# Moving parts of an on-chip float64 conversion from GpSimd to VectorE in a planned attention-and-MLP kernel

## The chip, the cores and the metric

The kernel runs on one core of a Trainium2 chip. The metric is device time in microseconds (us); three runs of the kernel before gave a median of 1079.98 us (1079.9 to 1080.02). The profile shows five engines of the core: TensorE (PE, with its weight loads as PEld), VectorE (DVE), ScalarE (ACT), GpSimd (POOL) and SyncE (SP), which here only issues transfers.

## The reference

A linear attention in the manner of Performer, followed by a two-layer MLP with an ELU between the layers. The attention's inputs are float32. The two weight matrices of the MLP come as float64.

```python
batch, n_heads, seq, head_dim = 8, 8, 576, 64      # 4608 tokens, 128 features
def phi(x):                                        # x is q or k, scaled
    h = einsum('bhsd,md->bhsm', x, omega) - sum(x * x, -1, keepdims=True) / 2
    return exp(h - max(h, -1, keepdims=True)) / sqrt(m)
kv  = einsum('bhsm,bhsd->bhmd', k_p, v)            # k_p = phi(k), q_p = phi(q)
z   = sum(k_p, axis=2)
x   = einsum('bhsm,bhmd->bhsd', q_p, kv) / (einsum('bhsm,bhm->bhs', q_p, z)[..., None] + 1e-06)
# x becomes 4608 x 512, heads side by side
h   = x @ w_in                                     # 512 x 2048
g   = where(h > 0, h, exp(min(h, 0)) - 1)
out = g @ w_out                                    # 2048 x 512
```

## The kernel before

**Attention** is done by pairs of heads, 32 pairs (`i` from 0), four to a batch entry. A pair's k is projected into `ppk` (the transposes and products on PE; minimum, exponent and so on elsewhere), its features are `hk`; `kv` multiplies them with v into `pkv` and sums them into `z`; q is projected into `ppq`, its features are `hq`. `finish` spreads z over the partitions (`pz`), forms the denominators on VectorE (L652 and the reciprocal at L661, tile `den`), divides `hq` by them ("norm", a tensor_tensor at L350), transposes it on PE (`pt`, L673), copies it to `qh`, multiplies with kv into `pn` (L700), and splits the result into a high part `xh` (ScalarE) and a low part `xl` (VectorE, L713). The first pairs project plain float32 x in four-pass matmuls (L457); from pair 7 of k and pair 8 of q on, x is split first into two parts (`tk`, `tq`; a tensor_tensor at L350) and projected by L507.

**MLP.** The tokens are worked in 12 blocks of 384; d_ff is worked in 16 steps of 128. A step F of layer 1 takes 12 matmuls (L830 to L832: high times high, high times low, low times high, for four chunks of 128 of the model's width) into `ph`, ScalarE and VectorE make the ELU `e` (L839, L840, L843), and `e` is split into `g`, high (a copy at L345 or L347) and low (a tensor_tensor at L350). Layer 2 multiplies g with w2 into three accumulators, nine matmuls for a step (L864 to L866). Blocks 0 to 2 are done in two halves of d_ff each, the rest whole. Block 0 needs the pairs 0 to 3; block 1 needs the pairs 4 to 7 as well, the chunk c of its steps the pair 4 + c.

**Conversion.** The weights are 32 tiles of 128x512 float64 words (16 of w1, 16 of w2). `from_f64` loads a tile into `raw` (L752, 512 KB), ScalarE scales its upper word into `u` (L755) and its lower one in place (L759), then come a clamp (L763, a tensor_scalar on VectorE or GpSimd), a shift (L770) and a sign (L775) on VectorE, an integer add on GpSimd (L778), the high part (a copy by ScalarE or VectorE, L345 or L347, into `w1c` or `w2h`) and the low part, the tail (`w1c` or `w2l`, a tensor_tensor at L350). w1's two parts are also written to DRAM (`w1s`, L802) for the later blocks, which load them from there (L805). Step f of block 0 needs w1's tile f, and its layer 2 w2's tile f.

**Order.** Nothing is ordered by hand. Every operation is recorded with an engine, a duration by a formula, a due time and its dependencies (`op`), and `Plan.order` deals them out: each engine, when free, starts the earliest due operation that is ready. Some operations carry alternatives (`alt`); `ALT` says how many us later (or earlier, if negative) the other engine is taken to be. `mine` decides whether the engine that asks should have the operation. The planner also holds VectorE and GpSimd apart for operations marked `port` (`held`). Each tag of `Buf` has a number of buffers, and a tile waits for one of them to come free. The kernel then runs each engine's list in that order, each instruction waiting on semaphores for its inputs.

Of the kernel before, what the change touches and what calls it, by code (L numbers as in the profile page):

```python
# [98 lines left out]
class Plan:  # L99
# [167 lines left out]
ALT = dict(kv=1, out=2, conv_clamp=-1, conv_hi=-1, conv_sub=2, g_hi=0, g_lo=1, y_hi=None, y_lo=-1, norm=2, turn=2, x_hi=2, sq=0)  # L267
# [24 lines left out]
def performer_elu_kernel(  # L292
# [102 lines left out]
    def load_pair(i, due):  # L395
# [7 lines left out]
        for nm, nat, mixed in (("k", k, kx), ("q", q, qx)):  # L403
            if native(i, nm):
                t = s["x" + nm] = Buf(sb, [P, 2, S], F32, "ld" if nm == "k" else "t", f"x{nm}_{i}", 2)
# [174 lines left out]
    def kv_sums(i, due, p, parts):  # L580
# [25 lines left out]
        def add(n, d, dst, x, y, reads):  # L606
            op("POOL", pool(n), d, lambda: nc.gpsimd.tensor_tensor(dst(), x(), y(), ALU.add), reads, (z,))

        add(4 * M, due + 0.1, lambda: z(), lambda: h()[:, 0:4], lambda: h()[:, 4:8], parts)
        add(2 * M, due + 0.2, lambda: z()[:, 0:2], lambda: z()[:, 0:2], lambda: z()[:, 2:4], (z,))  # L610
        for a in range(2):
# [3 lines left out]
                lambda r=r: h()[r, 8], [*parts, z],  # L615
            )

    def finish(i, due):
# [110 lines left out]
    def from_f64(src, hi, lo, nm, due, key):  # L729
# [19 lines left out]
        def ui():  # L749
# [13 lines left out]
            lambda e: (nc.vector if e == "DVE" else nc.gpsimd).tensor_scalar(  # L763
                u(), u(), -F64_MAX, F64_MAX, ALU.max, ALU.min
            ),
# [250 lines left out]
```

## Time and profile before

| | |
|---|---|
| median of three runs | 1079.98 us |
| the profiled execution | 1078.17 us, of which a span of 1076.3 us between first and last instruction |
| PE, ACT, DVE, POOL busy | 1050.0, 731.6, 601.5, 474.4 us |
| mean granted clock of TensorE | 0.99 |

The profile's groups name a line, an engine, an operation and its tiles (output first), then the count, the busy time, the mean duration of one in ns and the idle time of the engine before it with what ended it. Where a line is that of a helper (L345 and L347 for copies, L350 for every tensor_tensor by `tt`), the tile names tell the operations apart. Two records stand in the trace for one float32 matmul of the projections and of the products with kv.

### The profile page before, as it was taken

The numbers are of one execution on the slowest core, as the hardware profiler recorded it, in microseconds if no ns is written. First come the engines' busy times: TensorE is split into PE (matmuls) and PEld (weight loads), VectorE is DVE, ScalarE is ACT, GpSimd is POOL, SyncE is SP. The second block draws the span as 40 slices with busy tenths as digits, with TensorE's granted clock in tenths as the row PEclk, the third lists the DMA queues.
The fourth block names the chain that finished last, engine by engine and source line by source line (L and its number), as shares of the span: only waits on it lengthen the run. The fifth ranks groups of instructions, "written<-read, shape, count | busy, mean of one in ns | idle before, by whom it ended". The sixth has DMA issues, their size and how long they took to land.

```text
span 1076.3 us, 19179 instructions
## 1 busy us (share of the span) xinstructions
PE 1050.0 (98%) x6043; PEld 916.2 (85%) x6043; DVE 601.5 (56%) x2343; ACT 731.6 (68%) x1949; POOL 474.4 (44%) x466
## 2 busy tenths in 40 slices
PE   7999699999999999999999999999999999999998
PEld 7777589898888888998888888898888888898987
DVE  5788889755776754235666665224566665322221
ACT  6987775547977985347889998427899988432222
POOL 4677666753443554223454345223344554322221
PEclk8999899999999999999999999999999999999999
DMA  6555477657553553435455545444545542253431
GB/s 196 155 178 191 166 255 258 227 211 234 187 194 128 185 170 128 166 118 168 170 169 156 170 150 177 149 135 134 180 138 177 167 153 98 98 167 131 153 125 62
DMA packets 53237, 176.92 MB, mean 164 GB/s; under 512 B 6032, under 2 KB 6224, under 8 KB 53136
## 3 DMA queue, kind: packets, MB, share of 16 engines
q1 hardware_dynamic: 53136, 175.69, 49.3%
q8 instruction: 49, 0.80, 0.3%
q14 instruction: 52, 0.43, 0.1%
HBM read 155.48 MB, written 20.19 MB: 163 GB/s over the span
## 4 chain that ended last, share of the span: by engine, by line
PE 83%; ACT 5%; DVE 5%; DMA 3%; POOL 2%; issue 2%; SPq 0%; POOLq 0%; DVEq 0%; ACTq 0%
PE acc L864 12%; PE ph L830 11%; PE acc L866 11%; PE acc L865 11%; PE ph L832 11%; PE ph L831 11%; PE ppq L507 2%; PE pt L673 2%; PE pkv L591 2%; PE pn L700 2%; PE ppk L507 2%; DMA xk<-in_kx_dram 1%; PE ppq L457 1%; ACT hk L427 1%; ACT hq L427 1%
## 5 line engine op out<-in xcount | busy, mean ns | idle before, releaser
L350 POOL TENSOR_TENSOR g<-e,g 128x384 fp32r<-128x384 f32 x176 | 186.4, 1059 | 450.5 <-DVE g L347 333.3
L830 PE MATMUL ph<-xh,w1c 128*128 128x384 f32 x768 | 266.6, 347 | 0.8 <-DVE e L843 0.8
L832 PE MATMUL ph<-xh,w1c 128*128 128x384 f32 x768 | 258.3, 336 | 0.0
L831 PE MATMUL ph<-xl,w1c 128*128 128x384 f32 x768 | 258.0, 336 | 0.0
L843 DVE SCALAR_TENSOR_TENSOR e<-e,ph 128x384 f32<-128x384 f32 x192 | 106.2, 553 | 247.5 <-ACT e L840 244.0
L839 ACT ACTIVATE e<-ph 128x384 f32<-128x384 f32 x192 | 94.7, 493 | 216.1 <-PE ph L832 209.7
L864 PE MATMUL acc<-w2h,g 128*128 128x512 f32 x576 | 235.1, 408 | 0.7 <-ACT o L345 0.7
L865 PE MATMUL acc<-w2l,g 128*128 128x512 f32 x576 | 228.3, 396 | 0.0
L866 PE MATMUL acc<-w2h,g 128*128 128x512 f32 x576 | 228.2, 396 | 0.0
L830 PEld LDWEIGHTS ph<-xh,w1c 128*128 128x128 f32 x768 | 144.5, 188 | 15.6 <-issue 5.1
L831 PEld LDWEIGHTS ph<-xl,w1c 128*128 128x128 f32 x768 | 144.6, 188 | 8.0
L832 PEld LDWEIGHTS ph<-xh,w1c 128*128 128x128 f32 x768 | 144.0, 188 | 0.0
L866 PEld LDWEIGHTS acc<-w2h,g 128*128 128x128 f32 x576 | 108.6, 189 | 25.7
L864 PEld LDWEIGHTS acc<-w2h,g 128*128 128x128 f32 x576 | 108.6, 189 | 17.6 <-issue 4.1
L865 PEld LDWEIGHTS acc<-w2l,g 128*128 128x128 f32 x576 | 108.9, 189 | 11.7
L840 ACT ACTIVATE e<-e 128x384 f32<-128x384 f32 x192 | 101.6, 529 | 3.4
L525 DVE CUSTOM_DVE_ANT_0 hq<-ppq,p2q 128x128 f32<-128x128 f32 x216 | 54.1, 288 | 63.4 <-ACT p2q L516 62.4
L350 POOL TENSOR_TENSOR hq<-hq,den 128x512 f32<-128x512 f32 (+1 forms) x93 | 81.0, 884 | 10.2 <-DVE den L661 8.5
L525 DVE CUSTOM_DVE_ANT_0 hk<-ppk,p2k 128x128 f32<-128x128 f32 x225 | 56.3, 287 | 45.6 <-ACT p2k L516 41.1
L652 DVE CUSTOM_DVE_ANT_0 junk<-hq,pz 128x128 f32<-128x128 f32 (+1 forms) x320 | 73.5, 280 | 10.6 <-PE pz L633 8.2
L516 ACT ACTIVATE p2q<-ppq,sqq 128x128 f32<-128x128 f32 x216 | 67.5, 369 | 14.0 <-PE ppq L507 13.3
L516 ACT ACTIVATE p2k<-ppk,sqk 128x128 f32<-128x128 f32 x225 | 67.4, 365 | 7.1 <-PE ppk L507 6.9
(94 smaller groups left out, 1619.5 us busy)
## 6 DMA issues: line engine op xcount, KB each, us to landing
w1c<-w1s SPq DMA_DIRECT2D x176, 512.0 KB, 3.3
raw_w<-in_w_dram SPq DMA_DIRECT2D x32, 512.0 KB, 4.2
xk<-in_kx_dram SPq DMA_DIRECT2D x25, 576.0 KB, 4.2
xq<-in_qx_dram SPq DMA_DIRECT2D x24, 576.0 KB, 4.6
v<-in_v_dram SPq DMA_DIRECT2D x32, 325.0 KB, 3.6
out_dram<-o SPq DMA_DIRECT2D x36, 256.0 KB, 2.6
w1s<-w1c SPq DMA_DIRECT2D x16, 512.0 KB, 3.3
xq<-in_q_dram SPq DMA_DIRECT2D x8, 288.0 KB, 3.9
```

The lines of the kernel that those rows point to most:

```text
L350: (nc.vector if e == "DVE" else nc.gpsimd).tensor_tensor(*args)
L516: nc.scalar.activation(p2()[:, a], view()[:, a, M:], AF.Identity, bias=sq()[:, j:j + 1], scale=1.0)
L525: nc.vector.tensor_tensor_reduce(out=h()[:, j, :], in0=view()[:, a, 0:M], in1=p2()[:, a, :], scale=1.0, scalar=HIGHEST, op0=ALU.add, op1=A ...
L830: nc.tensor.matmul(ph(), wh, xh[:, c, o:o + TB], start=(c == 0), stop=False)
L831: nc.tensor.matmul(ph(), wh, xl[:, c, o:o + TB], start=False, stop=False)
L832: nc.tensor.matmul(ph(), wl, xh[:, c, o:o + TB], start=False, stop=(c == NC - 1))
L839: op("ACT", act(TB, True), due, lambda: nc.scalar.activation(e(), ph(), AF.Relu, scale=-1.0), (p,), (e,))
L840: op("ACT", act(TB), due + 0.2, lambda: nc.scalar.activation(e(), e(), AF.Exp, scale=-1.0), (e,), (e,))
L843: lambda: nc.vector.scalar_tensor_tensor(e(), e(), -1.0, ph(), ALU.add, ALU.max), (p, e), (e,),
L864: nc.tensor.matmul(a(), g()[:, 0, ts], w2h[:, f], start=(f == f0), stop=False)
L865: nc.tensor.matmul(a(), g()[:, 0, ts], w2l[:, f], start=False, stop=False)
L866: nc.tensor.matmul(a(), g()[:, 1, ts], w2h[:, f], start=False, stop=(f == f1 - 1))
```

## The change

Seven edits in one:

- The clamp of the conversion is VectorE's alone; before, GpSimd could take it.
- The conversion's tail goes to VectorE first; GpSimd takes it only if that ends 1 us sooner by the planner's reckoning. Before, it was GpSimd's, with VectorE 2 us behind.
- The low part of `g` in block 0's steps goes to VectorE first; in the other blocks it stays GpSimd's first.
- `mine` now counts the time for which the other of VectorE and GpSimd holds the two apart.
- `raw` has four buffers, not three. The z sums of the pairs from 8 on, and the kv that is transposed there, which had two buffers of their own each, now lie in buffers of `raw`.
- The x of k (and the x of q that is split) has three buffers, not two.
- `qh`, the turned q, has one buffer, not two.

Line numbers of the changed kernel are some 5 to 14 higher: L457 is L462 there, L507 L512, L673 L686, L700 L713, L713 L726, L763 to L778 are L776 to L788, L830 to L832 are L840 to L842, L843 is L853, L864 to L866 are L878 to L880, and the helpers L345, L347 and L350 are L350, L352 and L355.

```diff
 # Plan.order, mine(n, eng): when would the other engine e end this operation?
-                t = max(free[e], now, ready[n][e]) + ns + late * 1e3
+                t = max(free[e], now, ready[n][e])
+                if e == "POOL":
+                    t = max(t, held["DVE"])
+                elif e == "DVE" and tasks[n][6]:
+                    t = max(t, held["POOL"])
+                t += ns + late * 1e3
...
-ALT = dict(kv=1, out=2, conv_clamp=-1, conv_hi=-1, conv_sub=2, g_hi=0, g_lo=1, y_hi=None, y_lo=-1, norm=2, turn=2, x_hi=2, sq=0)
+ALT = dict(kv=1, out=2, conv_hi=-1, conv_sub=1, g_hi=0, g_lo=1, g_lo0=1, y_hi=None, y_lo=-1, norm=2, turn=2, x_hi=2, sq=0)
...
 # load_pair: x of k, x of q
-                t = s["x" + nm] = Buf(sb, [P, 2, S], F32, "ld", f"x{nm}_{i}", 2)
+                t = s["x" + nm] = Buf(sb, [P, 2, S], F32, "ld", f"x{nm}_{i}", 3)
...
 # kv_sums: z and the kv to be transposed
-        z = s["z"] = Buf(sb, [P, 4, M], F32, "zs", f"zs_{i}", 2)
-        kvt = Buf(sb, [P, M], F32, "kvt", f"kvt_{i}", 2)
+        zt = s["z"] = Buf(sb, [P, 2 * 512], I32, "raw", f"zs_{i}", 4)
+        ktk = (zt, "kvt")
...
 # finish
-        qh = Buf(sb, [P, 2, S], F32, "qh", f"qh_{i}", 2)
+        qh = Buf(sb, [P, 2, S], F32, "qh", f"qh_{i}", 1)
...
 # from_f64
-        raw = Buf(sb, [P, 2 * 512], I32, "raw", f"raw_{nm}", 3)
+        raw = Buf(sb, [P, 2 * 512], I32, "raw", f"raw_{nm}", 4)
...
             "DVE", dve(512, True), due - 6,
-            lambda e: (nc.vector if e == "DVE" else nc.gpsimd).tensor_scalar(
-                u(), u(), -F64_MAX, F64_MAX, ALU.max, ALU.min
-            ),
-            (u,), (u,), alt=other("conv_clamp", "POOL", 1885), port=True,
+            lambda: nc.vector.tensor_scalar(u(), u(), -F64_MAX, F64_MAX, ALU.max, ALU.min), (u,), (u,), port=True,
...
-            "POOL", pool(512), due - 3,
+            "DVE", dve(512), due - 3,
             lambda e: tt(e, lo(), u(), hi().bitcast(F32), ALU.subtract), (u, key + ("h",)), (key + ("l",),),
-            alt=other("conv_sub", "DVE", dve(512)), port=True,
+            alt=other("conv_sub", "POOL", pool(512)), port=True,
...
 # layer1: the low part of g
-        op(
-            "POOL", pool(TB), due + 1.5,
+
+        first, second = ("POOL", pool(TB)), ("DVE", dve(TB))
+        if not blk:
+            first, second = second, first
+        op(
+            *first, due + 1.5,
```

What the edits do to the order is seen at two places. The first is PE's list around pair 7, the last pair that block 1 needs: `pt_7` are the transposes of its q, `pn_7` its products with kv, `ph_F` and `acc` the MLP's layers (g_5 is the g of step 5). Before:

```order
L866 MATMUL acc_0_0_2_951<-w2h_79,g_5_1440 128x512
...
L673 MATMUL pt_7_0_1576<-ident_67,hq_7_1414 128x128 x4
L673 MATMUL pt_7_1_1588<-ident_67,hq_7_1414 128x128 x4
L673 MATMUL pt_7_2_1601<-ident_67,hq_7_1414 128x128
...
L700 MATMUL pn_7_0_1615<-qh_7_1584,kvf1_78 64x256 x2
L700 MATMUL pn_7_256_1618<-qh_7_1584,kvf1_78 64x320 x2
...
L830 MATMUL ph_7_1651<-xh_83,w1c_7_1625 128x384
```

and now:

```order
L686 MATMUL pt_7_0_1593<-ident_67,hq_7_1456 128x128 x4
L878 MATMUL acc_0_0_0_951<-w2h_79,g_5_1430 128x512
...
L840 MATMUL ph_7_1610<-xh_83,w1c_7_1559 128x384
...
L878 MATMUL acc_0_0_0_951<-w2h_79,g_6_1584 128x512
...
L840 MATMUL ph_8_1652<-xh_83,w1c_8_1561 128x384
...
L686 MATMUL pt_7_1_1671<-ident_67,hq_7_1456 128x128 x4
L686 MATMUL pt_7_2_1677<-ident_67,hq_7_1456 128x128
...
L713 MATMUL pn_7_0_1697<-qh_7_1606,kvf1_78 64x256 x2
L713 MATMUL pn_7_256_1700<-qh_7_1606,kvf1_78 64x320 x2
```

Ahead of `pn_7` PE had 84 matmuls of `ph` and 54 of `acc` in its list, and now has 105 and 63: layer 1 of step 7, three quarters of step 8 and layer 2 of one more step have moved ahead of it; the attention's rows ahead of it are the same.

The second place is VectorE's list at the same pair: `dens` of pair 7 (the rows with junk_7), the norm of `hq_7`, and the conversion of the tiles that the next steps need. Before:

```order
L661 RECIPROCAL den_7_1504<-den_7_1504 128x1
L843 SCALAR_TENSOR_TENSOR e_6_1534<-e_6_1534,ph_6_1480 128x384
L770 TENSOR_SCALAR u_w1_7_1433<-u_w1_7_1433 128x512
L770 TENSOR_SCALAR u_w2_6_1494<-u_w2_6_1494 128x512
L775 SCALAR_TENSOR_TENSOR u_w1_7_1433<-raw_w1_7_1397,u_w1_7_1433 128x512
L775 SCALAR_TENSOR_TENSOR u_w2_6_1494<-raw_w2_6_1443,u_w2_6_1494 128x512
L350 TENSOR_TENSOR hq_7_1414<-hq_7_1414,den_7_1504 128x512 x2
L350 TENSOR_TENSOR hq_7_1414<-hq_7_1414,den_7_1504 128x128
L350 TENSOR_TENSOR g_6_1557<-e_6_1534,g_6_1557 128x384
```

and now:

```order
L853 SCALAR_TENSOR_TENSOR e_6_1522<-e_6_1522,ph_6_1441 128x384
L674 RECIPROCAL den_7_1531<-den_7_1531 128x1
...
L355 TENSOR_TENSOR w2l_80<-u_w2_5_1262,w2h_79 128x512
L355 TENSOR_TENSOR w1c_7_1559<-u_w1_7_1365,w1c_7_1559 128x512
L352 CAST w2h_79<-u_w2_6_1445 128x512
L355 TENSOR_TENSOR g_6_1584<-e_6_1522,g_6_1584 128x384
L355 TENSOR_TENSOR w2l_80<-u_w2_6_1445,w2h_79 128x512
L776 TENSOR_SCALAR u_w2_7_1600<-u_w2_7_1600 128x512
L776 TENSOR_SCALAR u_w2_8_1614<-u_w2_8_1614 128x512
```

The norm of pair 7 has left VectorE's list (it is in GpSimd's now), the tails of w2's tiles 5 and 6 and of w1's tile 7 have come in, and the shifts and signs of w1's tile 7 and w2's tile 6 stand further ahead, before the denominators. Of the 32 tails all were GpSimd's, and 31 are VectorE's now; of the 32 clamps 8 were GpSimd's and none is. Of the 192 low parts of `g` VectorE had 16 and has 23.

More of the change, by code (lines that the diff above doesn't have):

```diff
@@ L404, in load_pair @@
             if native(i, nm):
[L405 removed]
+                t = s["x" + nm] = Buf(sb, [P, 2, S], F32, "ld" if nm == "k" else "t", f"x{nm}_{i}", 3 if nm == "k" else 2)
                 dma(lambda t=t: t()[0:D], nat[i], P * S * 4, (t, 0), (t, 1))
             else:
[L408 removed]
+                t = s["x" + nm] = Buf(sb, [P, 2, S], F32, "ld", f"x{nm}_{i}", 3)
                 dma(lambda t=t: t(), mixed[i - NNAT[nm]], P * S * 8, (t, 0), (t, 3))
@@ L583, in kv_sums, with z, kvt @@
         h, v, kvf = s["hk"], s["v"], kvs[i % 2]
-        z = s["z"] = Buf(sb, [P, 4, M], F32, "zs", f"zs_{i}", 2)
-        kvt = Buf(sb, [P, M], F32, "kvt", f"kvt_{i}", 2)
+        zt = s["z"] = Buf(sb, [P, 2 * 512], I32, "raw", f"zs_{i}", 4)
+        ktk = (zt, "kvt")
+        def z():
+            return zt().bitcast(F32)[:, 0:4 * M].rearrange("p (t m) -> p t m", m=M)
+        def kvt():
+            return zt().bitcast(F32)[:, 4 * M:5 * M]
         def mms():
@@ L596, in kv_sums @@
         op(
-            "ACT", act(M, True), due + 2.2, lambda e: copy(e, kvt(), p()[:, 0:M]), ((p, 0),), (kvt,),
+            "ACT", act(M, True), due + 2.2, lambda e: copy(e, kvt(), p()[:, 0:M]), ((p, 0),), (ktk,),
             alt=other("kv", "DVE", dve(M)),
         )
-        op("PE", 109, due + 2.5, lambda: nc.tensor.transpose(p()[:, M:2 * M], kvt(), ident), (kvt,), ((p, 1),))
+        op("PE", 109, due + 2.5, lambda: nc.tensor.transpose(p()[:, M:2 * M], kvt(), ident), (ktk,), ((p, 1),))
         op(
@@ L606, in add @@
         def add(n, d, dst, x, y, reads):
-            op("POOL", pool(n), d, lambda: nc.gpsimd.tensor_tensor(dst(), x(), y(), ALU.add), reads, (z,))
+            op("POOL", pool(n), d, lambda: nc.gpsimd.tensor_tensor(dst(), x(), y(), ALU.add), reads, (zt,))
         add(4 * M, due + 0.1, lambda: z(), lambda: h()[:, 0:4], lambda: h()[:, 4:8], parts)
-        add(2 * M, due + 0.2, lambda: z()[:, 0:2], lambda: z()[:, 0:2], lambda: z()[:, 2:4], (z,))
+        add(2 * M, due + 0.2, lambda: z()[:, 0:2], lambda: z()[:, 0:2], lambda: z()[:, 2:4], (zt,))
         for a in range(2):
@@ L614, in kv_sums @@
                 M, due + 0.3 + 0.1 * a, lambda r=r, a=a: z()[r, a], lambda r=r, a=a: z()[r, a],
-                lambda r=r: h()[r, 8], [*parts, z],
+                lambda r=r: h()[r, 8], [*parts, zt],
             )
@@ L632, in sums @@
         def sums():
-            nc.tensor.matmul(pz()[:, 0:2 * M], ones, z()[:, 0:2].rearrange("p a m -> p (a m)"), start=True, stop=True)
+            nc.tensor.matmul(pz()[:, 0:2 * M], ones, z().bitcast(F32)[:, 0:2 * M], start=True, stop=True)
         if i < NONES:
@@ L848, in layer1 @@
         op(*first, due + 1.2, lambda x: copy(x, g()[:, 0], e()), (e,), ((g, 0),), alt=other("g_hi", *second), port=True)
+        first, second = ("POOL", pool(TB)), ("DVE", dve(TB))
+        if not blk:
+            first, second = second, first
         op(
-            "POOL", pool(TB), due + 1.5,
+            *first, due + 1.5,
             lambda x: tt(x, g()[:, 1], e(), g()[:, 0].bitcast(F32), ALU.subtract), (e, (g, 0)), ((g, 1),),
-            alt=other("g_lo", "DVE", dve(TB)), port=True,
+            alt=other("g_lo" if blk else "g_lo0", *second), port=True,
         )
```

## The prediction

> **What bounds the kernel now.** I read the page's busy times first, then a table by stage, which shows the clock too.
>
> ```profile
> PE 1050.0 (98%) x6043; PEld 916.2 (85%) x6043; DVE 601.5 (56%) x2343; ACT 731.6 (68%) x1949; POOL 474.4 (44%) x466
> ...
> 0.00:50.00 50.00, 43.17 (x314) 37.98 (x314) 33.94 (x132) 39.54 (x113) 26.62 (x29) 0.93 0.63 187
> 50.00:95.00 45.00, 41.96 (x288) 34.66 (x288) 38.54 (x115) 38.58 (x103) 34.74 (x28) 1.00 0.54 172
> 95.00:150.00 55.00, 43.37 (x226) 34.43 (x226) 46.28 (x147) 41.40 (x104) 32.90 (x25) 0.88 0.55 187
> 150.00:200.00 50.00, 49.33 (x248) 44.26 (x247) 42.53 (x71) 31.52 (x63) 32.87 (x27) 1.00 0.71 250
> 200.00:1076.00 876.00, 872.18 (x4974) 764.88 (x4972) 440.19 (x1882) 580.56 (x1571) 347.23 (x361) 1.00 0.47 156
> ```
>
> The columns of the last five are the stretch, its length, busy time of PE, PEld, DVE, ACT and POOL, the granted clock, the DMA share. From 200 us on PE idles 3.8 us in 876; nothing saved on another engine there can be worth more than that. The head is another matter: 6.8, 3.0 and 11.6 us of idle up to 150, and the clock at 0.93 and 0.88. What the change is worth is decided before 150, above all from 95 on, where DVE is busy 84% of the time, ACT 75%, POOL 60%. Since PE is full afterwards, a microsecond won there should arrive at the end.
>
> What PE waits for in that stretch, from its timeline and waits, and what the clock does:
>
> ```profile
> 98.26 0.43 PE L630 MATMUL pz<-ident,z 128*128 128x128 f32 x2 [1.69 <-ACT kvf L345]
> 98.97 1.19 PE L700 MATMUL pn<-qh,kvf 128*64 128x256 f32 x8 [0.28 <-ACT qh L345]
> ...
> 110.97 1.09 PE L673 MATMUL pt<-ident,hq 128*128 128x128 f32 x4 [2.89 <-DVE mnk L525]
> ...
> 130.02 0.66 PE L673 MATMUL pt<-ident,hq 128*128 128x128 f32 x4 [3.40 <-DVE hq L350]
> ...
> PE pt L673 <- DVE hq L350: 4.5, 2, 3.4
> PE ppq L457 <- ACT hk L427: 4.1, 2, 2.4
> PE pt L673 <- DVE mnk L525: 3.4, 3, 2.9
> ...
> 100.00:103.80 3.80, 3.80 (x11) 2.96 (x10) 3.35 (x21) 2.56 (x6) 3.36 (x3) 0.55 0.74 214
> 110.50:114.00 3.50, 3.03 (x14) 3.06 (x15) 1.74 (x10) 2.65 (x8) 2.21 (x2) 0.51 0.38 142
> 131.00:138.00 7.00, 5.60 (x20) 3.37 (x21) 6.48 (x22) 4.58 (x14) 2.92 (x3) 0.51 0.89 359
> ```
>
> Each longer stall (1.69, 2.89, 3.40 us) is followed by a stretch at half clock, in which PE is busy and slow. Taking busy time times the lost half, they cost 3.80 x 0.45 + 3.03 x 0.49 + 5.60 x 0.49 = 1.7 + 1.5 + 2.7 = 5.9 us.
>
> The chain of waits says what made DVE late before the worst of them:
>
> ```profile
> 120.69 0.07 POOL w2l L350
> 120.76 1.29 issue
> 122.05 1.02 POOL g L350
> ...
> 123.16 1.44 POOL tk L350
> ...
> 124.69 1.93 POOL u_w L763
> ...
> 128.34 1.54 issue
> 129.89 1.98 DVE hq L350 x2
> ```
>
> A tail of the conversion (0.07 and 1.29 us), a low part of g, a split of k's x and a clamp stand in a row on POOL; then DVE's norm of pair 7 waits another 1.54 us and runs, and PE's transposes with it.
>
> **The change part by part: what leaves POOL and comes to DVE.** The groups of the first 150 us, and single rows of DVE's timeline, alone and beside a POOL instruction:
>
> ```profile
> L763 POOL TENSOR_SCALAR u_w<-u_w 128x512 f32<-128x512 f32 x8 | 15.3, 1915 | 7.2 <-ACT u_w L755 7.0
> L350 POOL TENSOR_TENSOR w2l<-u_w,w2h 128x512 fp32r<-128x512 f32 x8 | 11.8, 1470 | 6.1 <-DVE w2h L347 6.1
> L350 POOL TENSOR_TENSOR w1c<-u_w,w1c 128x512 fp32r<-128x512 f32 x8 | 10.5, 1307 | 6.5 <-DVE w1c L347 3.5 <-PE pt L673 1.0 <-ACT w1c L345 0.8
> L350 POOL TENSOR_TENSOR g<-e,g 128x384 fp32r<-128x384 f32 x5 | 6.1, 1216 | 4.3 <-DVE g L347 3.5 <-ACT g L345 0.8
> ...
> L775 DVE SCALAR_TENSOR_TENSOR u_w<-raw_w,u_w 128x512 int32<-128x512 int32 x17 | 12.9, 766 | 0.0
> L770 DVE TENSOR_SCALAR u_w<-u_w 128x512 int32<-128x512 int32 x17 | 11.4, 681 | 0.6 <-POOL u_w L763 0.6
> L350 DVE TENSOR_TENSOR tk<-xk,tk 64x576 fp32r<-64x576 f32 x5 | 5.8, 1151 | 0.1
> L763 DVE TENSOR_SCALAR u_w<-u_w 128x512 f32<-128x512 f32 x9 | 5.1, 566 | 0.0
> L350 DVE TENSOR_TENSOR g<-e,g 128x384 fp32r<-128x384 f32 x4 | 4.3, 1064 | 0.0
> ...
> 107.83 0.42 DVE L770 TENSOR_SCALAR u_w<-u_w 128x512 int32<-128x512 int32 x1
> 108.17 1.64 DVE L350 TENSOR_TENSOR g<-e,g 128x384 fp32r<-128x384 f32 x1
> 114.41 0.68 DVE L775 SCALAR_TENSOR_TENSOR u_w<-raw_w,u_w 128x512 int32<-128x512 int32 x1
> 131.79 0.55 DVE L350 TENSOR_TENSOR g<-e,g 128x384 fp32r<-128x384 f32 x1
> ...
> 107.99 1.39 POOL L778 TENSOR_TENSOR u_w<-u_w,raw_w 128x512 int32<-128x512 int32 x1 [1.99 <-DVE u_w L775]
> ```
>
> Count up to step 8 of layer 1 (DVE's e_8, POOL's g_8), after which PE is full. From POOL go 8 clamps (15.3 us), 15 of the tails (8 x 1.47 + 7 x 1.31 = 20.9) and 3 low parts of g (3.6); to it come 4 squares of k's x, 2 norms, a split and an add, which I put at 1.2 to 1.5 us each by the rows above, 9 to 11. POOL loses about 30 of the 94 us that the table gives it up to 150.
>
> DVE gets 8 clamps at 0.42 us, 16 tails, whose nearest row is the sign of the same 128x512 size at 0.68, and 3 low parts of g at 0.55: 3.4 + 10.9 + 1.6 = 15.9 us. It loses a norm's two pieces, two splits, three pieces of k's features and two copies, about 6 us. Net +10, if nothing holds it.
>
> It is held, though: g took 0.55 us alone and 1.64 beside an add of 1.39 on POOL. Mean less lone duration times count, over L770, L763, L775, g and tk, is 17 x 0.26 + 9 x 0.15 + 17 x 0.09 + 4 x 0.51 + 5 x 0.40 = 11.3 us (lone, tk is put at 0.75: from g's 384 elements in 0.55 to the sign's 512 in 0.68 it is 1 ns an element). With copies, norms and the rest, 79 instructions in all, I put the time held at 16. POOL's time falls to 64/94; DVE's instructions of that sort rise to about 100: 16 x 0.68 x 1.27 = 14, so 2 less. DVE net: +8 us. The lower bound of what that costs is 0 (DVE idles 31 us before 150), the upper 8. Of PE's three large waits above, DVE is named in two, with 7.9 of 12.0 us, but part of that was POOL's hold; I take half, **-4**.
>
> [...]
>
> **The last pair.** Behind pt_7_0 PE now has 21 matmuls of layer 1 and 9 of layer 2 that came after pn_7 before, by
>
> ```profile
> 137.92 0.34 PE L831 MATMUL ph<-xl,w1c 128*128 128x384 f32 x1
> 138.10 0.34 PE L832 MATMUL ph<-xh,w1c 128*128 128x384 f32 x1
> ...
> 149.12 0.23 PE acc L866
> ```
>
> 21 x 0.18 + 9 x 0.23 = 5.8 us of work. It fills what was idle from 131 to 138 (1.4 us) and, if the clock then stays, the 2.7 lost to it: up to **+4.1**, nothing if the conversions come no earlier. They should: the chain's clamp and tail (3.3 us of POOL) are 1.1 us of DVE now, and a fourth word buffer lets a load go out before an add frees the third. I take 4.1. The norm of pair 7 goes to POOL, out of the queue in which it stood behind two signs and a hold: between 0 and the 3.4 us of its stall; half, **+1.7**.
>
> A new wait comes in: the first of that filler, layer 2 of step 5, needs w2's tail 5, and DVE has it behind pair 7's denominators, e_6 and two pieces of pair 8. Queued behind it are w1's tail 7, the low part g_6 and w2's tail 6, for which steps 7 and 6 wait in turn. I take the tail and one piece as long as g's, 0.68 + 0.55, against pt_7_0's 0.66 on PE: **-0.6**; the upper end is the stall of 3.4 us come back.
>
> **The earlier stalls**, 1.69 and 2.89 us, with 1.7 and 1.5 of half clock behind them, are 7.8 us. Both stand behind DVE instructions held by POOL. Between 0 and 7.8; I take POOL's lost third, **+2.5**.
>
> **Edits at nothing.** k's x in three buffers, qh in one, the z sums among the word buffers act mostly after 200 us, where PE's 3.8 us of idle is all there is to lose or win; work of other pairs and blocks covers them. If that cover goes, a pair's copies to qh wait for the pn before, 1.19 us a pair by the row at 98.97. SP issues the word loads earlier, past loads of k and v. Four squares of k's x go from ACT to POOL at the start, for better or worse by under 1 us.
>
> **The sum:** 4.1 + 1.7 + 2.5 - 4.0 - 0.6 = 3.7 us. The profiled execution took 1078.17 us, 1.87 of it around the span of 1076.3, so 1074.5; the median of the runs lies 1.8 above it: 1076.3.
>
> **Rivals.** (1) DVE becomes the bound before 150. The earlier stalls stay, the filler wins its 4.1 less the new wait's 3.4, and half of the 8 us lands on the path: 1080 + 4 - 0.7 = 1083.3; all of it makes 1087.3. For it: 84% busy, in order, and held as above. Against: 31 us of idle, and 30 us off POOL. It decides from the point where DVE puts more on the path than the filler wins, 0.7 us in this case, 7.7 if the other gains come.
> (2) The stalls only move: what is won at pair 7 is lost at pairs 5 and 6, where DVE now has tails between denominators. 1080, give or take 2.
> (3) PE never idles long enough to lose its clock after 95: all 5.9 us, 1.4 of idle at pair 7 and half of the 4.6 us of the two earlier stalls, less 1 for DVE: 8.6 us, 1071.4. For it: the filler. Against: the new wait at the same place. [...]
> (4) The change doesn't do what it says: the order shows 31 tails and 8 clamps moved, so only the buffers can be idle; no chance of its own.
>
> **How the numbers follow.** Forecast, 2 to 7 us faster: 0.43. Rival 3: 0.14. Rival 2: 0.22. Rival 1: 0.21. The three runs shown lie within 0.12 us; I take 0.2%, 2.2 us, as what can be told from no change. Faster 0.57, the same 0.22, slower 0.21. The likeliest time is 1076.3 us, its own range 1073 to 1078; the range with the rivals, leaving out the far end of 1 and 3, is 1069.5 to 1083.5.
>
> **What would show it.** Right: PE's idle from 95 to 150 falls from 11.6 us to about 7, the clock there rises over 0.88, DVE's busy share rises, POOL's falls by a fifth or more, and after 200 us nothing differs by more than 1 us. Wrong: DVE over 92% busy from 95 to 150 with PE's waits naming tails, or idle that turns up before 95 or after 150 instead.

## The result, and the profile after

The changed kernel takes 1073.5 us (median of 20 runs, 1068.5 to 1079.5) against 1080.0 for the kernel before (20 runs, 1077.5 to 1084.4): a ratio of 0.9937, 95% interval 0.9923 to 0.9952, which is 5.2 to 8.3 us. The forecast was 1076.3, a gain of 3.7.

The execution of the changed kernel that was profiled with this comparison happened to be the longest of its 20 (1079.48 us); so a second profile of the same kernel, of 1070.3 us (its rerun in the experiments), stands beside it.

The busy times and the table by stage of the changed kernel, first profile (columns as in the prediction: PE, PEld, DVE, ACT, POOL, granted clock, DMA share):

```profile
PE 1050.2 (97%) x6043; PEld 921.0 (85%) x6043; DVE 605.5 (56%) x2380; ACT 731.6 (68%) x1952; POOL 415.8 (39%) x426
...
0.00:50.00 50.00, 41.00 (x297) 36.72 (x298) 31.69 (x120) 36.64 (x104) 19.63 (x24) 0.90 0.71 184
50.00:95.00 45.00, 40.83 (x262) 33.51 (x260) 39.85 (x129) 35.37 (x96) 23.37 (x21) 0.92 0.54 172
95.00:150.00 55.00, 47.55 (x260) 39.76 (x259) 50.15 (x155) 40.78 (x106) 21.14 (x18) 0.88 0.59 208
150.00:200.00 50.00, 49.06 (x247) 44.19 (x246) 36.04 (x66) 29.03 (x55) 19.42 (x14) 1.00 0.67 224
200.00:1076.00 876.00, 871.80 (x4986) 766.84 (x4984) 447.73 (x1916) 589.76 (x1593) 332.23 (x351) 1.00 0.47 157
```

and of the same kernel, second profile:

```profile
PE 1044.1 (98%) x6043; PEld 915.1 (86%) x6043; DVE 605.0 (57%) x2380; ACT 730.5 (68%) x1952; POOL 417.8 (39%) x426
...
0.00:50.00 50.00, 43.93 (x331) 37.72 (x331) 36.59 (x147) 42.06 (x122) 24.20 (x29) 1.00 0.72 210
50.00:95.00 45.00, 40.50 (x268) 33.45 (x265) 41.89 (x112) 35.41 (x93) 22.15 (x19) 0.96 0.53 172
95.00:150.00 55.00, 47.42 (x259) 40.38 (x260) 47.40 (x151) 42.06 (x104) 20.37 (x18) 0.91 0.62 227
150.00:200.00 50.00, 48.53 (x242) 43.10 (x240) 39.05 (x68) 25.52 (x49) 23.04 (x15) 1.00 0.65 226
200.00:1066.00 866.00, 863.67 (x4947) 760.44 (x4947) 440.11 (x1905) 585.46 (x1586) 328.02 (x347) 1.00 0.46 155
```

In both, PE's idle time from 95 to 150 us is 7.5 us (7.6 in the second), where it was 11.6, and POOL has lost 30 (28) of its 94 us up to 150. But before 95 PE idles 13.2 us in the first and 10.6 in the second, where it was 9.8, so that over the first 200 us it idles 21.6 and 19.6 us against 22.2: of the 4 us saved in one stage most is back in others in the first profile, and more than a third in the second. What differs more between the two is the clock: 0.90, 0.92 and 0.88 in the first three stages of the one, 1.00, 0.96 and 0.91 of the other. These figures count the clock as full until the trace's first record of it, at 4.8 us before, 5.0 in the first profile and 9.97 in the second. It is not full until then: in the second profile the 20 records of `ppk` that run before 9.97 us take 4.38 us from end to end and 421 ns each (each starts before the one ahead of it has ended), and in the other two, after 5 us, 2.39 us and 275 ns; in a stretch that the trace records at half clock (11.6 to 15.0 us before) eight such records of `ppq` take 420 ns each. With the start counted in, PE is at half clock for 25.3 us before, 35.7 in the first profile and 23.6 in the second, all of it up to 150 us. (Of the "four-pass" matmuls of plain float32 the trace of before shows this, from 15 to 95 us: two records for 128 columns, 112 ns from start to start at the median, where one for 384 columns in layer 1 takes 174; that is 3.9 times as long a column.)

The groups of the conversion in the first 150 us of the changed kernel, first profile (line, engine, operation, tiles, count, busy us and mean ns, idle before):

```profile
L785 DVE SCALAR_TENSOR_TENSOR u_w<-raw_w,u_w 128x512 int32<-128x512 int32 x17 | 12.4, 732 | 0.1
L780 DVE TENSOR_SCALAR u_w<-u_w 128x512 int32<-128x512 int32 x17 | 9.6, 571 | 0.0
L776 DVE TENSOR_SCALAR u_w<-u_w 128x512 f32<-128x512 f32 x17 | 9.4, 563 | 0.1
L355 DVE TENSOR_TENSOR g<-e,g 128x384 fp32r<-128x384 f32 x7 | 7.2, 1028 | 0.0
L355 DVE TENSOR_TENSOR w2l<-u_w,w2h 128x512 fp32r<-128x512 f32 x9 | 6.5, 721 | 0.0
...
L355 DVE TENSOR_TENSOR w1c<-u_w,w1c 128x512 fp32r<-128x512 f32 x7 | 5.6, 799 | 0.0
```

A tail takes 0.72 to 0.80 us on VectorE where it took 1.31 to 1.47 on GpSimd; the clamp takes 0.56 where GpSimd took 1.92.

PE's longer waits around the last pair, and a stretch behind or across them, from the timeline and the table of stretches of the first profile,

```profile
112.35 0.36 PE L512 MATMUL ppk<-om,tk 128*128 128x256 f32 x1 [1.51 <-DVE mnk L530]
...
131.04 0.60 PE L512 MATMUL ppk<-om,tk 128*128 128x256 f32 x2 [1.76 <-ACT hq L432]
132.90 0.80 PE L512 MATMUL ppk<-om,tk 128*128 128x256 f32 x2 [1.26 <-DVE den L665]
134.27 1.09 PE L686 MATMUL pt<-ident,hq 128*128 128x128 f32 x4 [0.57 <-ACT g L350]
...
131.00:138.00 7.00, 5.13 (x16) 4.27 (x17) 6.91 (x32) 6.31 (x15) 2.85 (x3) 0.52 1.01 401
```

and of the second:

```profile
119.09 0.63 PE L462 MATMUL ppq<-of,xq 128*64 128x128 f32 x4 [1.72 <-DVE xl L726]
123.04 0.80 PE L512 MATMUL ppk<-om,tk 128*128 128x256 f32 x2 [1.21 <-ACT hq L432]
124.90 0.80 PE L512 MATMUL ppk<-om,tk 128*128 128x256 f32 x2 [1.06 <-DVE den L665]
...
119.00:126.00 7.00, 4.34 (x15) 3.03 (x15) 6.84 (x33) 4.79 (x11) 4.22 (x4) 0.51 0.86 325
```

The stall of 3.40 us at pair 7's norm is gone: `pt` now waits 0.57 us (in both profiles), for something else. In its place stand waits of 1.1 to 1.8 us, and a stretch at half clock is still there. So from 95 to 150 us idle time was saved, but little of the clock: the time at half clock there was 13.7 us and is 13.7 and 10.2.

**Where the time went.** Stages by the clock on the wall hold different work in different kernels. A point at which all kernels have done nearly the same work is the first matmul of layer 1's step 48 (the 577th of its matmuls; 88 products `pn` and 408 matmuls of layer 2 are done by then in every one of the 14 profiles). It is not quite the same: where k's x has three buffers (the changed kernel and runs 1, 3, 4, 7, 8 and 10), one pair's product of k's features with v (`pkv`) more is done by then, 100 records against 80 and 5 transposes against 4, which take PE 1.2 us. The time of that point, and the time from there to the start of step 191, the last, worked out from the timelines:

| us | to step 48 | step 48 to 191 |
|---|---|---|
| before | 332.8 | 729.4 |
| after, first profile | 337.6 | 726.1 |
| after, second profile | 328.8 | 725.7 |

Two things show. Up to step 48 one and the same kernel differs by 8.8 us between these two executions, and from there on by 0.4: their difference lies in the head, where the clock comes and goes. Up to step 48 PE idles 23.1 us in the first and 20.4 in the second, and half of the time at half clock is 17.9 and 11.8: 2.7 and 6.1 us, together the 8.8. And after step 48, where PE idles under 1 us in these three profiles and where the prediction put nothing, the changed kernel needs 3.5 us less, of which 1.2 are the product done earlier: some 2.3 us have been won.

### The profile page after: what moved, and what is told of

It reads as the page before. It is cut to its first block, busy times and chain, and to the rows that moved or that the text cites. A ratio compares the mean times of both kernels' runs of the same rounds, so it can differ in the third digit from the quotient of the medians.

```text
span 1077.7 us, 19141 instructions
## 1 busy us (share of the span) xinstructions
PE 1050.2 (97%) x6043; PEld 921.0 (85%) x6043; DVE 605.5 (56%) x2380; ACT 731.6 (68%) x1952; POOL 415.8 (39%) x426
## 4 chain that ended last, share of the span: by engine, by line
PE 81%; DVE 7%; ACT 7%; DMA 4%; issue 2%; SPq 0%; POOL 0%; DVEq 0%; ACTq 0%
PE ph L840 11%; PE ph L842 11%; PE ph L841 11%; PE acc L878 11%; PE acc L879 11%; PE acc L880 11%; PE pt L686 3%; PE pn L713 3%; PE ppq L512 3%; PE pkv L604 2%; PE ppk L512 2%; ACT hk L432 1%; DMA part<-o 1%; DMA xk<-in_k_dram 1%; PE pz L646 1%
## 5 line engine op out<-in xcount | busy, mean ns | idle before, releaser
L355 POOL TENSOR_TENSOR g<-e,g 128x384 fp32r<-128x384 f32 x169 | 177.3, 1049 | 458.0 <-DVE g L352 353.4
L840 PE MATMUL ph<-xh,w1c 128*128 128x384 f32 x768 | 268.1, 349 | 2.5 <-DVE e L853 1.8
L842 PE MATMUL ph<-xh,w1c 128*128 128x384 f32 x768 | 259.7, 338 | 0.0
L853 DVE SCALAR_TENSOR_TENSOR e<-e,ph 128x384 f32<-128x384 f32 x192 | 106.1, 553 | 248.9 <-ACT e L850 243.8
L878 PE MATMUL acc<-w2h,g 128*128 128x512 f32 x576 | 233.6, 406 | 0.0
L880 PE MATMUL acc<-w2h,g 128*128 128x512 f32 x576 | 226.0, 392 | 0.0
L840 PEld LDWEIGHTS ph<-xh,w1c 128*128 128x128 f32 x768 | 145.2, 189 | 19.0 <-issue 4.7
L842 PEld LDWEIGHTS ph<-xh,w1c 128*128 128x128 f32 x768 | 144.7, 188 | 0.0
L880 PEld LDWEIGHTS acc<-w2h,g 128*128 128x128 f32 x576 | 108.4, 188 | 24.7 <-DVE g L355 0.3
L878 PEld LDWEIGHTS acc<-w2h,g 128*128 128x128 f32 x576 | 108.6, 189 | 16.0 <-issue 3.9
L355 POOL TENSOR_TENSOR hq<-hq,den 128x512 f32<-128x512 f32 (+1 forms) x96 | 86.1, 912 | 20.6 <-DVE den L674 17.1
L788 POOL TENSOR_TENSOR u_w<-u_w,raw_w 128x512 int32<-128x512 int32 x32 | 47.0, 1473 | 67.9 <-DVE u_w L785 38.8
```

The lines of the kernel that those rows point to most:

```text
L355: (nc.vector if e == "DVE" else nc.gpsimd).tensor_tensor(*args)
L840: nc.tensor.matmul(ph(), wh, xh[:, c, o:o + TB], start=(c == 0), stop=False)
L842: nc.tensor.matmul(ph(), wl, xh[:, c, o:o + TB], start=False, stop=(c == NC - 1))
L853: lambda: nc.vector.scalar_tensor_tensor(e(), e(), -1.0, ph(), ALU.add, ALU.max), (p, e), (e,),
L878: nc.tensor.matmul(a(), g()[:, 0, ts], w2h[:, f], start=(f == f0), stop=False)
L880: nc.tensor.matmul(a(), g()[:, 1, ts], w2h[:, f], start=False, stop=(f == f1 - 1))
```

## The experiments

All ratios are to the kernel before, timed beside it on the same chip, with their 95% intervals; 0.001 is 1.08 us.

**1. The changed kernel again.**

> The changed kernel once more, nothing edited. Of the 20 runs of it the profiled one was the slowest (1079.48 us, granted clock 0.985; the median is 1073.53), so its trace is not a typical one. If the spread of 11 us comes from how many stretches at half clock an execution meets in the head, a trace of a faster execution has the same order and the same work, a granted clock of 0.989 or more, and the missing time in fewer stretches of 0.5; the time goes as the runs did, 0.8 us for each 0.001 of the clock. If the spread has another cause (transfers at the start), the clock is the same and the time is lost or won before 50 us. Time about 1073.5, 6.5 below the kernel before.

0.9947 (0.9928 to 0.9967), 1073.5 against 1078.5 us. This is the yardstick for the runs with it.

**2 and 3. The engines' moves alone, and the buffers alone.** First the changed kernel with the buffers of before (the moves and the planner's rule stay; the edits of the buffers are given in words):

```diff
-  raw 4 buffers, z sums and transposed kv in raw; x of k 3; qh 1
+  raw 3 buffers, zs 2, kvt 2; x of k 2; qh 2
```

> All the moves between VectorE and GpSimd and the planner's rule of the changed kernel, but the buffers as before: three for float64 words, own ones for the z sums and the transposed kv, two of x, two of qh. If the gain is the clamps and tails off GpSimd (my forecast), 4 us or more below the kernel before. If the fourth word buffer makes it, within 2 us of the kernel before. If it takes both, in between or slower than before.

0.9956 (0.9940 to 0.9971): a gain of 4.8 us (3.1 to 6.5) from the order alone. Then the kernel before with the new buffers:

```diff
-  raw 3 buffers, zs 2, kvt 2; x of k 2; qh 2
+  raw 4 buffers, z sums and transposed kv in raw; x of k 3; qh 1
```

> The buffers of the changed kernel alone: clamps, tails, low parts of g and the planner's rule as before. If the moves make the gain, within 2 us of the kernel before; if the fourth word buffer and the third x make it, 4 us or more below; if it takes both, within 2 us or slower.

1.0053 (1.0036 to 1.0070), 5.7 us slower. By step 48 the two fall apart: the buffers alone reach it at 344.9, 12.1 us late, but then need only 724.3 us, 5.1 less than before (1.2 of it the product done earlier); the moves alone reach it at 328.8, 4.0 early, and then need 729.8, as before. So the engines' moves act in the head, the buffers in both, there for the worse and afterwards for the better; the sizes in the head come from one profile each, where two executions of one kernel differed by 8.8 us. The two don't add up: -4.8 and +5.7 us alone, -6.8 together. With the moves alone VectorE is nearly full from 95 to 150 us, 52.00 of 55, and still the kernel is faster; the row of that stage:

```profile
95.00:150.00 55.00, 45.06 (x244) 35.52 (x243) 52.00 (x161) 45.71 (x118) 24.54 (x21) 0.97 0.65 223
```

**4. The tails back to GpSimd**, in the changed kernel:

```diff
-  "DVE", dve(512), due - 3, ... alt=other("conv_sub", "POOL", pool(512))     # conv_sub=1
+  "POOL", pool(512), due - 3, ... alt=other("conv_sub", "DVE", dve(512))     # conv_sub=2
```

> The changed kernel with the tails on GpSimd first again (VectorE 2 us behind), all else changed. If the tails are the part that matters, most of the gain goes: 1077 to 1081. If the clamps, the planner's rule or the buffers make it, the time stays near the changed kernel's, 1072 to 1076.

0.9945 (0.9925 to 0.9965): no difference to the changed kernel that these runs can tell (their intervals are some 2 us wide to each side), though all 32 tails are GpSimd's again, and VectorE's clamps take longer, 0.89 us each over the whole span in place of 0.61 and 0.57 in the changed kernel's two profiles. The groups of that kernel over the whole span:

```profile
L776 DVE TENSOR_SCALAR u_w<-u_w 128x512 f32<-128x512 f32 x32 | 28.4, 893 | 4.4 <-ACT u_w L768 4.4
L355 POOL TENSOR_TENSOR w1c<-u_w,w1c 128x512 fp32r<-128x512 f32 x16 | 23.2, 1447 | 14.7 <-DVE w1c L352 7.4 <-issue 1.9 <-PE pn L713 1.8
L355 POOL TENSOR_TENSOR w2l<-u_w,w2h 128x512 fp32r<-128x512 f32 x16 | 22.6, 1416 | 16.1 <-DVE w2h L352 16.1
```

The largest move of the change is not what earns, given the others; alone, in the kernel before, it was not tried.

**5 and 7. The clamps.** Alone, in the kernel before:

```diff
-  lambda e: (nc.vector if e == "DVE" else nc.gpsimd).tensor_scalar(...), (u,), (u,), alt=other("conv_clamp", "POOL", 1885)
+  lambda: nc.vector.tensor_scalar(...), (u,), (u,)
```

> The kernel before with one edit: the clamps are VectorE's alone. The move of the tails turned out not to be what gains (with the tails back on GpSimd the changed kernel kept its time). If the clamps are what gains, 4 to 6 us below the kernel before, since a clamp of 1.92 us on GpSimd stands on the chain ahead of the worst stall and takes 0.42 to 0.57 on VectorE. If the planner's rule gains, within 2 us of the kernel before.

1.0062 (1.0045 to 1.0079), 6.7 us slower. PE's waits in its timeline, and the table of the stretch behind them:

```profile
130.69 1.12 PE L673 MATMUL pt<-ident,hq 128*128 128x128 f32 x4 [3.70 <-DVE hq L350]
...
139.15 0.98 PE L507 MATMUL ppk<-om,tk 128*128 128x256 f32 x3 [2.47 <-DVE mnk L525]
...
130.00:144.00 14.00, 10.17 (x35) 7.77 (x36) 12.40 (x34) 9.76 (x25) 7.68 (x5) 0.52 0.45 179
```

The norm of pair 7 stays on VectorE here, its stall grows from 3.40 to 3.70 us, a second one of 2.47 follows, and 14 us pass at half clock where it was 7. The reverse, the clamps allowed to GpSimd again in the changed kernel (11 of the 32 go there; `conv_clamp=-1` is back in `ALT`):

```diff
-  lambda: nc.vector.tensor_scalar(...), (u,), (u,)
+  lambda e: (nc.vector if e == "DVE" else nc.gpsimd).tensor_scalar(...), (u,), (u,), alt=other("conv_clamp", "POOL", 1885)
```

> The changed kernel, but GpSimd may take clamps again as before (11 of 32 then go there, the tails stay on VectorE). If the clamps gain, most of the 6 us goes: 1077 to 1080. If the rule or the tails do, the time stays at 1072 to 1075.

0.9976 (0.9956 to 0.9996): 3 to 4 us of the gain are lost, by run 1 or by the first comparison; the interval is clear of the first comparison's (up to 0.9952), but not quite of run 1's (up to 0.9967). So the same edit costs 6.7 us alone and earns 3 to 4 with the others.

**6 and 8. The planner's rule**, alone in the kernel before (this edit), and taken out of the changed kernel (its reverse), with the lines of the conditions drawn together:

```diff
-  t = max(free[e], now, ready[n][e]) + ns + late * 1e3
+  t = max(free[e], now, ready[n][e])
+  if e == "POOL": t = max(t, held["DVE"])
+  elif e == "DVE" and tasks[n][6]: t = max(t, held["POOL"])
+  t += ns + late * 1e3
```

> The kernel before with one edit: the planner counts the time for which the other of VectorE and GpSimd holds the two apart; clamps, tails and buffers may go where they could before. If the rule gains, 4 to 6 us below the kernel before; if the clamps gain, within 2 us or slower.

> The changed kernel without the planner's rule. If the rule gains, most of the 6 us goes: 1077 or more. If the clamps do, the time stays at 1072 to 1075.

1.0004 (0.9991 to 1.0017) and 0.9952 (0.9935 to 0.9970): worth nothing that can be told either way.

**9. What the buffers do after step 48.** The start-to-start time of layer 2's matmuls after 200 us (from one to the next; for the last of a sum, where another of layer 2 follows), worked out from the timelines, has two values in the kernels so far. Its medians for the three matmuls of a sum (high g by high w2, high by low, low by high) are 233, 234 and 233 ns with the buffers of before, whatever the order, and 229, 232 and 226 ns with the new buffers. The instructions there are the same, and so are the tiles w2h, w2l, xh and xl; but the tiles of the pool behind k's x have other addresses, g among them. So the kernel before was given one tile more, never used, of 128 bytes, just ahead of g; six small tiles behind g move with it, and the order of all instructions on PE, VectorE, ScalarE and GpSimd is that of before:

```diff
+PAD = dict(g=32)
...
             pool, shape, dtype, name = self.args
+            if self.key in PAD:
+                pool.tile([P, PAD.pop(self.key)], F32, tag="pad_" + self.key, bufs=1, name="pad_" + self.key)
             self.tile = pool.tile(shape, dtype, tag=self.key, bufs=self.n, name=name)
```

> The kernel before with one tile more in its pool: 128 bytes per partition, never used, taken just ahead of the three buffers of g. The order of all instructions on every engine is that of before; only g (and six small tiles behind it) lies 128 bytes higher: g starts at 209,216 in place of 209,088 of a partition, which is 320 in place of 192 above a multiple of 512, as it is in the changed kernel. Theory (where g lies sets how fast the matmuls of layer 2 follow one another): after 200 us the three matmuls that sum a tile start 229, 232 and 226 ns after one another in place of 233, 234 and 233 (medians), those of layer 1 stay at 175, 174 and 174 ns, and the time falls by 576 sums x 7 to 10 ns = 4 to 6 us: 1074 to 1076, ratio 0.9945 to 0.9965. Rival (the pace comes from the other engines' new order, or from another tile's place): 233, 234, 233 ns as before and a ratio within 0.002 of 1.

0.9975 (0.9962 to 0.9989), 2.7 us faster (1.2 to 4.1), and the medians are 229, 232 and 226 ns. The groups of layer 1 and layer 2 between 200 and 1060 us, before:

```profile
L832 PE MATMUL ph<-xh,w1c 128*128 128x384 f32 x676 | 227.4, 336 | 0.0
...
L864 PE MATMUL acc<-w2h,g 128*128 128x512 f32 x503 | 204.8, 407 | 0.0
L866 PE MATMUL acc<-w2h,g 128*128 128x512 f32 x504 | 199.1, 395 | 0.0
L865 PE MATMUL acc<-w2l,g 128*128 128x512 f32 x503 | 198.7, 395 | 0.0
```

and with the 128 bytes (L837 is L832 there, L869 to L871 are L864 to L866):

```profile
L837 PE MATMUL ph<-xh,w1c 128*128 128x384 f32 x676 | 227.8, 337 | 0.0
...
L869 PE MATMUL acc<-w2h,g 128*128 128x512 f32 x504 | 204.1, 405 | 0.0
L870 PE MATMUL acc<-w2l,g 128*128 128x512 f32 x503 | 197.9, 394 | 0.0
L871 PE MATMUL acc<-w2h,g 128*128 128x512 f32 x503 | 197.0, 392 | 0.0
```

Unrounded, the means of layer 2 fall by 2.2, 1.5 and 3.5 ns, 7.2 ns for each of the 576 sums, 4.2 us; those of layer 1 rise by 0.2, 0.3 and 0.6 ns, 768 times, 0.8 us. That makes 3.3, within the interval of the difference measured. The expectation had put it at 4 to 6 because it did not allow for layer 1. In the one profile only 0.6 us of it shows between step 48 and step 191 (728.8 against 729.4): start to start, layer 2 takes 3.0 us less there and layer 1 2.1 more, and PE idles 1.1 us longer.

**10 to 12. Parts of the buffers, with g in one place and the other.** The changed kernel with three word buffers and own buffers for the sums, in which g happens to lie where it lay before:

```diff
-  raw 4 buffers, z sums and transposed kv in raw
+  raw 3 buffers, zs 2, kvt 2
```

> The changed kernel with three buffers for float64 words in place of four, and with the sums and their transposed copy in buffers of their own, as before; k's x keeps three buffers, turned q one. Here g lies at the addresses of the kernel before (209,088), w1's chunks lie 4,608 bytes higher than before. Theory (g's place sets layer 2's pace): after 200 us layer 2's matmuls start 233, 234, 233 ns apart as before, though all else is as in the changed kernel, and that costs 4 to 6 us: 1077 to 1079.5, ratio 0.997 to 0.9995; the third matmul of layer 1 at 177 or 174 ns tells whether the place of w1's chunks sets it. Rival (the fourth buffer for words is what gains, by earlier arrival of the weights): the pace of after (229, 232, 226) and a loss of 3 us or more before 150 us. By the prediction's own terms (the buffers at nothing): 1073.5, ratio 0.995, and no change of pace.

Medians 233, 234, 233 ns, as before, and layer 1's third at 174 ns though w1's chunks lie elsewhere: 0.9969 (0.9953 to 0.9984). Its rows of layer 2:

```profile
L872 PE MATMUL acc<-w2h,g 128*128 128x512 f32 x504 | 205.4, 408 | 0.0
L874 PE MATMUL acc<-w2h,g 128*128 128x512 f32 x504 | 199.2, 395 | 0.0
L873 PE MATMUL acc<-w2l,g 128*128 128x512 f32 x504 | 199.1, 395 | 0.0
```

It lacks 3.5 us to the changed kernel by the first comparison (0.9937) and 2.4 by run 1; g's place accounts for 2.7 of that, so nothing that can be told is left for the fourth buffer and the sharing. Then the changed kernel with two buffers for k's x and two for qh, g only 128 bytes below its place in the changed kernel:

```diff
-  x of k 3 buffers; qh 1
+  x of k 2 buffers; qh 2
```

> The changed kernel with two buffers for k's x and two for turned q, as before; four buffers for float64 words, shared with the sums, stay. Here g starts at 213,184, 128 bytes below the changed kernel's g and 192 above a multiple of 512 like the kernel before; w1's chunks start at 188,608, 192 above a multiple of 512 and of 1,024 like before (in the changed kernel 704 above a multiple of 1,024). Theory (g's place within 512 bytes sets layer 2's pace): 233, 234, 233 ns as before, 4 to 6 us lost: 1077 to 1079.5, ratio 0.997 to 0.9995. Rival 1 (the part of the memory counts, not the place within 512 bytes): 229, 232, 226 ns, time by the schedule alone, 1073.5 +-2. Rival 2 (k's third x is what gains after 200 us): the pace of after and a loss of 2 us or more spread after 200 us.

233, 234, 233 ns again, as the place within 512 bytes says, and 0.9954 (0.9939 to 0.9968), 1074.4 us, 2.6 us less than the expected range begins with. So either two buffers for k's x and two for qh are better by some 2 us than three and one, or the runs of this kernel fell well; the next run was to tell. Last, the same with 128 bytes ahead of g:

```diff
+PAD = dict(g=32)      # as in run 9
```

> The changed kernel with two buffers for k's x and two for turned q (the run before it) and 128 unused bytes ahead of g, so that g starts at 213,312, the very address it has in the changed kernel; the order of all instructions is that of the run without the 128 bytes. Theory (the place of g and the order add up): layer 2's matmuls 229, 232, 226 ns apart after 200 us and 2.7 us less than that run's 1074.4: 1071.7, ratio 0.992 to 0.994, 1 to 2 us below the changed kernel. Rival (the gain of g's place and of the two buffers don't add up, because the third x of k and the single turned q earn something of their own): 1073.5 or more, ratio 0.9945 or more, as the changed kernel.

229, 232, 226 ns, as expected; its profile needs 727.6 us from step 48 to 191 in place of 730.9. But in time it is 0.9947 (0.9928 to 0.9965), 1073.7 us: 0.7 us less than without the bytes by the medians of 12 and 8 runs, on two chips, where 2.7 were expected, and the interval holds both what the theory and what the rival gave. Whether the order and the place of g add up fully is not decided by this, nor did any version prove faster than the changed kernel.

All fourteen profiles by that pace (us from step 48 to 191):

| g starts, above a multiple of 512 bytes | layer 2's medians, ns | step 48 to 191, us |
|---|---|---|
| 192: before, runs 2, 5, 6, 10, 11 | 233, 234, 233 | 729.4, 729.8, 729.6, 729.8, 728.8, 730.9; mean 729.7 |
| 320: after, runs 1, 3, 4, 7, 8, 9, 12 | 229, 232, 226 | 726.1, 725.7, 724.3, 725.9, 728.4, 727.6, 728.8, 727.6; mean 726.8 |

(Run 6 had 234 for the last median.) Of all tiles in the memory only g's place, taken above a multiple of 512, 1,024 or 2,048 bytes, differs between every kernel of the one row and every kernel of the other. The times of the two rows touch (run 10 and run 9 both need 728.8), and seven of the kernels have the 1.2 us of `pkv` behind them; with that added back the means are 729.9 and 727.7, 2.2 us apart. What does not overlap is the time of layer 2's 1284 matmuls between the two steps, start to start: 306.3 to 307.0 us in the first row, 302.7 to 304.2 in the second. Layer 1's 1716 take 306.9 to 308.4 and 307.7 to 309.8.

## Why the prediction was right, and where not

The direction and the range were right, and 1073.5 lies 2.8 us below the forecast. By its steps:

- **What bounds the kernel.** "From 200 us on PE idles 3.8 us in 876; nothing saved on another engine there can be worth more than that" is true as it stands: the idle is 4.2 and 2.3 us in the changed kernel's two profiles. The step that failed is the one drawn from it, that the buffers are "edits at nothing" and that "after 200 us nothing differs by more than 1 us". It took PE's pace for fixed. Some 2 us were won between steps 48 and 191 alone with PE just as busy (the means of the table above, with the `pkv` added back), because g lies elsewhere. Of the gain of 6.8 us this is the part that the forecast lacks: run 9 puts it at 2.7 (1.2 to 4.1) for the whole kernel.
- **What leaves POOL and comes to DVE.** POOL's 64 us up to 150 came out at 64.1 and 66.7, the tails at 0.72 to 0.80 against 0.68 and a hold, the clamps at 0.56 against 0.42. Mean less lone duration over the five groups that the prediction used gives 10.8 us of hold in the first profile, where it gave 11.3 before, and the tails add 1.2; so the hold did not grow much, as it said. VectorE's busy time up to 150 rose by 2.9 and 7.1 us, where 8 were put. The 4 us that this was to cost can't be read off. Run 5 shows that such a cost can be real when nothing is gained for it: the clamps alone cost 6.7 us, with a longer stall at the norm of pair 7 in its profile, which fits rival 1.
- **The hold**, mean less lone duration, shows in the low part of g, 1.03 us on VectorE on the mean (first profile, up to 150 us) and 0.55 alone; the tails took only 0.04 and 0.12 us over the 0.68 put for them. What hold there is does not reach the end: run 4 takes 31 tails off VectorE again and the time does not move by what can be told, and in run 2 VectorE is 95% busy from 95 to 150 us and the kernel 4.8 us faster than before.
- **The last pair**, +4.1 for the filler. The idle fell from 11.6 to 7.5 us, as said (to about 7). The other part, 2.7 us of clock, came in neither profile in full: the clock from 95 to 150 is 0.88 and 0.91, where over 0.88 was to show the step right: missed in one and barely met in the other (half of the 13.7 us at half clock there before, and of 13.7 and 10.2 now, makes 0 and 1.7 us of gain). Waits of 1.7 us stand where the one of 3.4 stood, with a stretch at half clock again. Of the reasons given for conversions that come earlier, neither the tails on VectorE nor the fourth word buffer is needed by itself: the gain stays without the former (run 4), and without the latter it stays but for g's place (runs 2 and 10); both left out together were not tried. The clamps on VectorE carry about half of the gain (run 7).
- **Pair 7's norm to POOL**, +1.7: the stall named after it is gone, in both profiles; its price by itself was not tried.
- **The new wait for w2's tail**, -0.6: no wait for a tail is among PE's from 95 to 150 in the two profiles of the changed kernel. In run 2, with three word buffers, there are two, 1.6 us together:

```profile
PE ph L836 <- DVE w1c L355: 0.9, 1, 0.9
PE acc L873 <- DVE w2l L355: 0.7, 1, 0.7
```

- **The earlier stalls**, +2.5: the 2.89 us at 111 became 1.51, the 1.69 at 98 is gone. But the prediction's sign of being wrong, idle that turns up before 95, shows as well: 13.2 and 10.6 us for 9.8. In the first profile a wait of q's projection for k's features grew, from 2.4 us at most to 4.2; in the second it is 1.4 at most. The waits of the first 150 us, first and second profile:

```profile
PE ppq L462 <- ACT hk L432: 6.3, 2, 4.2
...
PE ppq L462 <- ACT hk L432: 2.6, 3, 1.4
```

Nor did the clock gain before 95: with the start counted in, PE is at half clock for 11.6 us there before, and for 22.1 and 13.4 in the two profiles. What the head is worth differs by 8.8 us between the two, so a term of 2.5 us can't be confirmed from one profile of each.
- **The sum.** The order was forecast to bring 3.7 us in all; with g in its old place run 2 measured 4.8 (3.1 to 6.5), and runs 10 and 11, which keep parts of the new buffers, 3.3 and 5.0. So the order's sum was right in size, and 2.7 us came from outside it. Its terms were not confirmed one by one: of 2.7 us of clock that it counted as won 0 and 1.7 came, and the 4 us that it counted as lost can't be seen. That they balanced is luck in part.
- **The rivals.** Rival 1's mark, DVE over 92% from 95 to 150, is passed in run 2 (95%, with the two waits for tails above) without harm, so it was not a good mark; its mechanism fits run 5. Rival 2's time (no gain) is out by the interval, though waits did in part only move. Rival 3's condition, the clock kept after 95, does not hold in the changed kernel's profiles. In run 8 it does (1.00 from 95 to 200), and in runs 11 and 12 up to 150 (1.00, then 0.97 to 200); they took 1074.0, 1074.4 and 1073.7 us, not the 1071.4 that the rival gave.

Open is which moves make the order's gain together. Each left out by itself, the tails, the rule, and the third x with the single qh made no difference that can be told; the clamps take part but cost alone; the low parts of g in block 0 and the norm's move, which follows from the planner, were not tried by themselves.

## What to carry to other kernels

When an edit changes the number or the size of buffers, compare the start-to-start time of the matmuls in a stage where TensorE is hardly ever idle: a difference there can be the tiles' place in memory (in run 9 the medians fell by 4, 2 and 7 ns, and the time by 2.7 us), and one unused tile tells it from the effect of the order. Where a planner deals out the work, an edit has no price of its own (the clamps: 6.7 us lost alone, 3 to 4 won with the others), so undo each part from the changed kernel as well as doing it alone. Where the clock comes and goes (here 8.8 us between two executions of one kernel, up to step 48), compare profiles at a point of equal work and not by stages, count every kind of work done by then, and don't price a microsecond in the head from one profile.

## What was not expected of the hardware

- **The place of g.** Shifting g by 128 bytes, from 192 to 320 above a multiple of 512, makes layer 2's matmuls follow 4, 2 and 7 ns sooner (medians, 233, 234, 233 to 229, 232, 226 ns), and where another of layer 1 follows the third of layer 1, which doesn't read g, it does so after 177 ns in place of 174. g is what these matmuls load as weights (in the profile of before 1728 loads of 128x128 in layer 2, the size of g's slices, 189 ns each). Six small tiles behind g moved with it in run 9. Why the place matters is open, and other places were not tried.
- **The scatter.** 20 runs of the changed kernel lie 11 us apart, and the longer ones have the lower granted clock (0.985 at 1079.48 us, 0.994 at 1068.48). In two executions of the same program the stretch at half clock after the same wait had different lengths. In the first profile of the changed kernel, from its timeline and its table of stretches:

```profile
64.92 0.49 PE L558 MATMUL pkv<-v,hk 128*128 128x130 f32 x2 [1.96 <-ACT hq L432]
...
66.00:73.00 7.00, 7.00 (x34) 6.45 (x33) 4.75 (x17) 4.29 (x11) 1.34 (x2) 0.53 0.76 245
```

In the second:

```profile
59.43 0.49 PE L558 MATMUL pkv<-v,hk 128*128 128x130 f32 x2 [1.95 <-ACT hq L432]
...
61.00:64.50 3.50, 3.50 (x16) 3.05 (x16) 2.57 (x6) 1.42 (x4) 0.39 (x1) 0.52 0.59 175
```

PE is busy throughout both stretches, and both follow a wait of less than 2 us. By the traces' own records of the clock they last 6.83 and 3.41 us; in the first profile and in that of before every stretch between two changes of the clock is a whole multiple of 3.41 us (3.41, 6.83, 10.24, 17.07, 34.13, 40.96, 75.09 and 938.67). What decides between one such unit of half clock and two after the same wait, these runs don't show.
